# Softmax weights left unnormalised in the first attention steps, fewer TensorE array forms, and another order of the last matmuls

## The chip, the cores and the metric

One core of one Trainium2 chip runs the whole program. The metric is the device time of one execution in microseconds, shown as the median of several runs. A profiled execution has a time of its own, and a span from its first to its last instruction.

## The reference

Three blocks follow one another in float32: attention over 4 x 8 heads of 576 positions, with a causal window of 128 and a linear bias by distance; a feed-forward block with a softmax and a layer norm inside (SoLU); and a gated one.

```python
def _attn_ref(q, k, v):                       # (4, 8, 576, 64)
    scores = scale * np.matmul(q, k.transpose(0, 1, 3, 2))
    mask = (rel >= 0) & (rel < window)        # window = 128
    scores = np.where(mask, scores + bias[None], -1000000000.0)
    scores = scores - np.max(scores, axis=-1, keepdims=True)
    attn = np.exp(scores)
    attn = attn / (np.sum(attn, axis=-1, keepdims=True) + 1e-09)
    return np.matmul(attn, v)

def _moe_ref(x, w_in, w_out, g_ln):           # x (2304, 512), w_in (512, 1024)
    h = x @ w_in
    sm = softmax(h)
    solu = h * sm
    ln = (solu - mu) / np.sqrt(var + 1e-06) * g_ln
    return ln @ w_out

def _moe2_ref(x, w_gate, w_val, w_out):       # w_gate (512, 1536)
    g = x @ w_gate
    return g * sigmoid(g) * (x @ w_val) @ w_out
```

The weights of the two feed-forward blocks arrive as 64-bit words and are decoded to float32 on the chip.

## The kernel before

Every float32 product with a weight is made of three matmuls: both operands are split into a high and a low part (`high`, L267, and `low`, L271), and high x low, low x high and high x high are summed in PSUM (`HALVES`).

**Attention** runs in 20 steps (`steps`, 4 batches of 5 query tiles; the fifth has 64 rows). A step has four pairs of heads; a pair is one unit. For each pair of units `score` (L428) issues a block of small matmuls on 64 x 32 parts of the array. `attend` (L468) then takes a unit through the row maximum with the bias (VectorE, L488), two exponentials (ScalarE, L493) whose row sums are written beside them, their inverse (VectorE, L498 and L499), the scaling of the weights by it (`normalize`: ScalarE L504 or GpSimd L506), two transposes on TensorE (L524), a copy of these to SBUF (`pt`, L531 and L534) and, for two units at a time, the matmuls with the values (`values`, L566), on halves of 64 columns of the array. Keys reach over two tiles: one product is with the tile before (`vt`), one with the difference of the two (`vd`, made by `differ`, L410). In fifth tiles the transposes and the products with the difference use 64 rows of the array. The result (`px`, in a PSUM bank) is split into high and low, which are the feature tiles of the next block.

**The first feed-forward block** needs both weights decoded: `decode` (L319) takes a piece through ScalarE (L306, L310), VectorE (L311, L312), GpSimd (L314), and its split (L268, L272 or L274). `up` (L657) multiplies a feature tile by the first weight in two halves; `flip` (L719) turns the normalised tile, by TensorE or, for tiles 4 to 13, by a DMA for which `halves_of` first separates the 16-bit halves of the words; `down1` (L771) multiplies by the second weight. The matmuls of both have line L653.

**The second feed-forward block** uses seven products per block of weights (`products`, L992, matmuls at L1007). At its end `prepare` (L1095) makes operands out of stored results, `steps_of` (L1152) sums them over six chunks into PSUM (L1169), and `drain` (L1178) adds the finished sums to the output tiles (L1183) and stores them. There are six such passes; each goes chunk by chunk, and in a chunk product by product.

**The order** on every engine is fixed when the program is built. Each of these functions is a generator that hands operations to an `Emitter` (L105); it keeps a planned time for every engine and takes the operation that can start first, by rank among those that could start at once. An operation may name several engines; the one that would end first, with a bias (`B_DVE`, `B_ACT`), is taken. Offsets (`O_...`, `R_...`, `PW_...`) shift ranks. An engine name with a plus marks a port that VectorE and GpSimd share in the plan. From the planned time `TOGETHER` on, TensorE work that uses parts of the array (`form` 1 and 2) is held back in favour of plain matmuls while fewer than `LEAST` such operations are ready and none has waited `PATIENCE` ns. On the chip each engine takes its instructions in the written order and waits on semaphores.

Of the kernel before, what the change touches and what calls it, by code (L numbers as in the profile page):

```python
# [44 lines left out]
PLB = 2  # L45
PTB = 4
# [4 lines left out]
R_FLIP = 0.751  # L51
R_DOWN = 3.0
PW_IN = [-0.63, -0.23, -0.29, -0.28, 0.25, 0.17, 0.43, 0.28]
# [5 lines left out]
O_MAX = 0.0  # L59
O_EXP = -0.005  # L60
O_INV = 0.0
O_TURN = 0.136
O_PT = -1.188
O_VAL = 0.0
O_X = 0.316
# [4 lines left out]
O_LN = -0.416  # L70
# [4 lines left out]
TOGETHER = 96722.643  # L75
PATIENCE = 36.086
# [151 lines left out]
def attention_then_two_ffns(ctx: ExitStack, tc: tile.TileContext, qk, v, w_in, w_out, g_ln, w2, ident_d, base_d, tri_d, out):  # L228
# [145 lines left out]
    def load(c):  # L374
# [19 lines left out]
        loaded[c] = yield dma(vt[c][0:n], v[b, t * P:t * P + n, :], 262144)  # L394
# [15 lines left out]
    def differ(c):  # L410

        n = P if steps[c][1] < 4 else 64
        yield vd_s
        vd[c] = at.tile([P, DM], F32, tag="vd", bufs=VDB, name="vd")
        yield prepped[c][1]
        x = yield ([(POOL, t_pool(DM), lambda: nc.gpsimd.tensor_sub(vd[c][0:n], vt[c][0:n], vt[c - 1][0:n])),
                    (DVEP, t_dve(DM), lambda: nc.vector.tensor_sub(vd[c][0:n], vt[c][0:n], vt[c - 1][0:n]))],
                   [loaded[c], loaded[c - 1]])
# [4 lines left out]
    px_of, pts = {}, {}  # L423
# [43 lines left out]

    def attend(u):  # L468
# [23 lines left out]
        for j, d in enumerate(ds):  # L492
            ex.append((yield (ACT, 93 + t_act(P, True, True), lambda j=j: nc.scalar.activation(  # L493
                e[0:n, j], e[0:n, j], AF.Exp, bias=st[0:n, j:j + 1], scale=-1.0,
                accum_out=sc[0:n, j:j + 1]), [d, ds[0]], 0.0, O_EXP)))

# [4 lines left out]
        def normalize(eng):  # L501
# [6 lines left out]
        x = yield (DVE, 360, invert, ex, 0.0, O_INV)  # L508
        em.give(bank_s, x, k)
        x = yield ([(DVEP, t_dve(2 * P), lambda: normalize(nc.vector)),  # L510
                    (ACT, 2 * (93 + t_act(P)), lambda: normalize(nc.scalar)),
                    (POOL, t_pool(2 * P), lambda: normalize(nc.gpsimd))], [x], 0.0, O_INV)
# [14 lines left out]
        em.give(e_s, x)  # L527
        w = 2 * n
        ys = []
        if t:  # L530
            ys.append((yield (DVE, t_dve(w), lambda: nc.vector.tensor_tensor(  # L531
                pt[0:n, 1, :, 0:n], tp[0:n, :, 0:n], tri[0:n, 1, 0:n].unsqueeze(1).to_broadcast([n, 2, n]), ALU.mult),
# [21 lines left out]
        if t:  # L554
            yield differed[c]

        def values():
            todo = [(r, late) for r in units for late in ((1, 0) if t else (0,))]
            if t == 4:
                todo.sort(key=lambda x: -x[1])  # L560
            for r, late in todo:
                kp = n if late else P
                for j in range(2):
                    h = 2 * r + j
                    src = vd[c] if late else vt[c - 1] if t else vt[c]
                    nc.tensor.matmul(px[j * 64:(j + 1) * 64, r, 0:n], src[0:kp, h * 64:(h + 1) * 64],  # L566
                                     pts[c * NPAIR + r][0:kp, late, j, 0:n], start=r == 0 and (late == 1 or t == 0), stop=(late == 0),
                                     skip_group_check=True)

        values.form = 2  # L570
        x = yield (PE, 100 + 450 * len(units), values, [loaded[c]], 0.0, O_VAL)
# [9 lines left out]
        if t:  # L581
            em.give(v_s, x)
            em.give(vd_s, x)
        t0 = b * S + t * P
        done = 0
        last = []
        while done < n:
# [6 lines left out]
            src = px[:, :, done:done + w]  # L594
            y = yield (high(hi, src, 4 * w, False), [x], 0.0, O_X)
            y = yield (low(lo, src, hi, 4 * w, False), [y], 0.0, O_X)
# [7 lines left out]
        em.give(bank_s, y, px_of[c])  # L604
# [345 lines left out]
    def part_y(p, kk):  # L950
        yield opened2[p]
        if p == 1:
# [4 lines left out]
        x = yield (DMA, 2600.0, lambda: nc.sync.dma_start_transpose(  # L957
            r.rearrange("p (a h) t -> p a (h t)", a=2).bitcast(U16), src), (), 2000.0)
# [97 lines left out]
    ob, ob_ok = {}, [[Done() for _ in range(HB)] for _ in range(2 * NPR)]  # L1056
    t4_done = [[Done() for _ in range(HB)] for _ in range(NPR)]
# [37 lines left out]
    def prepare(k, i):  # L1095
# [45 lines left out]
        else:  # L1141
            x1 = yield add(r[:, 1], r[:, 1], r[:, 0], ALU.subtract, [x])
            x4 = yield add(r[:, 2], r[:, 2], t2, ALU.subtract, [x])
            sa = yield from split(0, 3, r[:, 1:4], [x1, x4])
            ends = [sa]
# [6 lines left out]
    def steps_of(k):  # L1152
# [3 lines left out]
        for i in range(HB):  # L1156
            yield ob_ok[k][i]
            yield wo_ok[i]
            for j, name in enumerate(PASS[half]):
                for q in range(2):  # L1160
                    if i == 0:
                        bk[name, q] = yield bank_s
                    o = banks[bk[name, q]][:, 0:NH]
                    c = PROD[name][0] * 256 + q * P
                    w = wo[i][:, :, c:c + P]

                    def f(o=o, w=w, j=j, i=i):
                        for m, (b, a) in enumerate(HALVES):
                            nc.tensor.matmul(o, w[:, b], ob[k, i][a][:, j], start=i == 0 and m == 0, stop=i == HB - 1 and m == 2)  # L1169

                    x = yield (PE, 3 * 0.455 * NH, f)
                    last[name, q] = x
            em.give(w2_s, x)
# [108 lines left out]
```

## Time and profile before

| | |
|---|---|
| median of 3 runs | 747.87 us (747.63 to 748.11) |
| the profiled execution | 744.56 us |
| its span, first to last instruction | 742.8 us |
| TensorE busy | 708.3 us (95%), 5084 matmuls |
| VectorE, ScalarE, GpSimd busy | 544.5 (73%), 469.9 (63%), 257.0 us (35%) |
| chain that ended last | TensorE 34% of the span |

PE is TensorE, PEld its weight load, DVE VectorE, ACT ScalarE, POOL GpSimd, SP the engine that issues the transfers. Busy shares are means over stages; a stage is read from its own window. A matmul in float32 of an attention product stands in the trace as two records.

### The profile page before, as it was taken

How to read it: one execution, taken by the hardware profiler on the slowest of the kernel's cores; microseconds unless marked ns; L12 is line 12 of the kernel's file. 1: busy time of each engine (PE TensorE's matmuls, PEld its weight loads, DVE VectorE, ACT ScalarE, POOL GpSimd, SP SyncE). 2: the span in 40 equal slices, each digit the busy share in tenths (PEclk: the TensorE clock that was granted, in tenths of full speed). 3: DMA queues.
4: the chain of work that ended last, by engine and by line, in shares of the span. 5: the costliest groups of instructions: out<-in, count | busy, mean ns of one | idle time of the engine just before them, and what ended most of it. 6: DMA issues, size and time to landing. Idle time of an engine off the chain costs nothing. (4 is left out here: it accounts for less than half of the span.)

```text
span 742.8 us, 14409 instructions
## 1 busy us (share of the span) xinstructions
PE 708.3 (95%) x5084; PEld 627.8 (85%) x5084; DVE 544.5 (73%) x1499; ACT 469.9 (63%) x1146; POOL 257.0 (35%) x268
## 2 busy tenths in 40 slices
PE   3879979999999999998999999999999999999997
PEld 1547757767787888888999999999999999999997
DVE  4778985667566654989978776876763699887975
ACT  7899996777777675786657555555553564442531
POOL 3686674454565554550034231221310000110200
PEclk9999999999999999999999999999999999999999
DMA  8763216354454327255564445643431788786851
GB/s 269 219 194 112 86 52 171 107 143 108 115 150 115 93 72 171 72 141 122 162 206 163 163 135 181 188 165 145 151 108 64 273 344 295 253 288 203 288 181 64
DMA packets 92329, 121.34 MB, mean 163 GB/s; under 512 B 46432, under 2 KB 59104, under 8 KB 92256
## 3 DMA queue, kind: packets, MB, share of 16 engines
q1 hardware_dynamic: 92256, 120.42, 51.6%
q8 instruction: 40, 0.66, 0.4%
q14 instruction: 33, 0.27, 0.1%
HBM read 76.09 MB, written 34.34 MB: 149 GB/s over the span
## 5 line engine op out<-in xcount | busy, mean ns | idle before, releaser
L1007 PE MATMUL bank<-yt,w 128*128 128x384 f32 x1008 | 183.5, 337 | 3.2 <-ACT t L1028 2.2
L1007 PEld LDWEIGHTS bank<-yt,w 128*128 128x128 f32 x1008 | 175.4, 188 | 6.4 <-ACT set L1028 2.8
L314 POOL TENSOR_TENSOR db<-db,dw 128x512 int32<-128x512 int32 x52 | 71.1, 1369 | 187.4 <-DVE db L312 144.4
L1169 PE MATMUL bank<-w,wo 128*128 128x384 f32 x756 | 132.9, 336 | 0.0
L1169 PEld LDWEIGHTS bank<-w,wo 128*128 128x128 f32 x756 | 132.3, 188 | 0.2 <-DVE w L272 0.2
L653 PE MATMUL bank<-wout,lnT 128*128 128x512 f32 x432 | 102.3, 392 | 0.0
L1007 PE MATMUL bank<-shared,w 128*128 128x384 f32 x504 | 96.0, 340 | 1.5 <-ACT set L1028 0.8
L653 PEld LDWEIGHTS bank<-wout,lnT 128*128 128x128 f32 x432 | 80.4, 188 | 17.2 <-issue 0.5
L1007 PEld LDWEIGHTS bank<-shared,w 128*128 128x128 f32 x504 | 87.2, 188 | 5.8 <-ACT set L1028 2.5
L653 PE MATMUL bank<-shared,shared 128*128 128x512 f32 x288 | 82.9, 418 | 1.6 <-ACT shared L268 1.6
L493 ACT ACTIVATE e<-e,st 128x128 f32<-128x128 f32 (+1 forms) x160 | 62.6, 401 | 14.7 <-DVE st L488 12.5
L653 PEld LDWEIGHTS bank<-shared,shared 128*128 128x128 f32 x288 | 51.9, 195 | 13.6 <-ACT shared L268 2.4
L506 POOL TENSOR_TENSOR e<-e,st 128x256 f32<-128x256 f32 (+1 forms) x66 | 40.8, 622 | 42.4 <-DVE st L499 31.1
L268 ACT CAST w<-t 128x768 fp32r<-128x768 f32 (+2 forms) x33 | 26.4, 806 | 42.3 <-DVE t L1123 26.7
L306 ACT ACTIVATE dw<-dw 128x512 int32<-128x512 uint32 x52 | 35.1, 675 | 14.5 <-DMA dw<-w 11.5
L488 DVE CUSTOM_DVE_ANT_0 e<-bank,bias 128x128 f32<-128x128 f32 (+1 forms) x160 | 38.5, 282 | 4.9 <-PE bank L454 2.7
L454 PE MATMUL bank<-keys,raw 64*32 64x160 f32 (+1 forms) x1152 | 32.5, 322 | 9.2 <-DMA keys<-qk 9.1
L1033 DVE TENSOR_TENSOR set<-set,bank 128x384 f32<-128x384 f32 x34 | 18.8, 552 | 30.3 <-PE bank L1007 23.3
L268 ACT CAST w<-db 128x512 fp32r<-128x512 f32 (+1 forms) x48 | 27.0, 565 | 20.7 <-POOL db L314 16.1
L524 PE MATMUL bank<-ident,e 128*128 128x128 f32 (+1 forms) x160 | 28.8, 291 | 11.3 <-POOL e L506 4.8
L653 PE MATMUL bank<-shared 128*128 128x512 f32 x144 | 38.9, 392 | 0.0
L524 PEld LDWEIGHTS bank<-ident,e 128*128 128x128 f32 (+1 forms) x160 | 18.3, 146 | 24.2 <-POOL e L506 8.7
(109 smaller groups left out, 1237.9 us busy)
## 6 DMA issues: line engine op xcount, KB each, us to landing
dw<-w SPq DMA_DIRECT2D x36, 512.0 KB, 3.9
t<-ascr SPq DMA_DIRECT2D x21, 768.0 KB, 5.5
ascr<-set SPq DMA_DIRECT2D x34, 384.0 KB, 2.6
later<-ascr SPq DMA_DIRECT2D x15, 768.0 KB, 5.4
wo<-wscr SPq DMA_DIRECT2D x6, 896.0 KB, 6.8
lscr<-pl SPq DMA_DIRECT2D x20, 256.0 KB, 2.3
raw<-qk SPq DMA_DIRECT2D x19, 256.0 KB, 3.4
yscr<-ys SPq DMA_DIRECT2D x18, 256.0 KB, 2.2
```

The costliest lines, as they stand in the source:

```text
L268: return [(ACT, t_act(n, sbuf), lambda: nc.scalar.copy(hi, src)), (DVEP if sbuf else DVE, t_dve(n, sbuf), lambda: nc.vector.tensor_copy(hi ...
L306: r = yield (ACT, t_act(512), lambda: nc.scalar.activation(a, lw, AF.Copy, scale=2.0 ** -29), (), 0.0, O_DEC)
L314: x = yield (POOL, t_pool(512), lambda: nc.gpsimd.tensor_tensor(b.bitcast(I32), b.bitcast(I32), a, ALU.add), [x, r], 0.0, O_DEC)
L454: nc.tensor.matmul(banks[ks[r]][i:i + Q, o:o + w], raw[c][rows, 2 * qd + j, i:i + Q], kt[rows, 2 * qd + j, k0:k0 + w], start=True, stop=True)
L488: d = yield (DVE, t_dve(P), lambda j=j: nc.vector.tensor_tensor_reduce(e[0:n, j], sc[0:n, j * 256:j * 256 + P], bias[0:n, 2 * pr + j, bs], ...
L493: ex.append((yield (ACT, 93 + t_act(P, True, True), lambda j=j: nc.scalar.activation(e[0:n, j], e[0:n, j], AF.Exp, bias=st[0:n, j:j + 1], ...
L506: eng.tensor_tensor(e[0:n], e[0:n], st[0:n, 6:8].unsqueeze(2).to_broadcast([n, 2, P]), ALU.mult)
L524: nc.tensor.transpose(tp[:, j, 0:n], e[0:n, j], ident[0:n, 0:n])
L653: nc.tensor.matmul(o, terms[m][0], terms[m][1], start=(m == 0), stop=(m == len(terms) - 1))
L1007: nc.tensor.matmul(o, l, r, start=first and m == 0, stop=m == 5, skip_group_check=True)
L1033: g2 = yield (DVE, t_dve(NH), lambda: nc.vector.tensor_add(t[:, 1], t[:, 1], sb), [x3, u2], 0.0, O_FREE)
L1169: nc.tensor.matmul(o, w[:, b], ob[k, i][a][:, j], start=i == 0 and m == 0, stop=i == HB - 1 and m == 2)
```

## The change

Four parts, all in one program.

In the first four steps (`SUMS = 4`) the exponentials are transposed and multiplied with the values as they are. The row sums of a step are collected in one SBUF tile (`rs`); after the last unit, two small VectorE operations invert all eight. TensorE multiplies each column of inverses, repeated over 64 columns, with the identity: that spreads them over the layout of `px` in a second bank. The bank is copied to SBUF (`rec`), multiplied by `px`, and the split into high and low reads `rec`. The bank of the scores is given back after the maximum instead of after the inverse.

Fifth tiles use full 128 x 128 transposes and value matmuls over 128 rows; the host pads `v` with zeros to 640 rows per batch, and whole tiles are loaded.

In the last pass, the last two chunks go product by product instead of chunk by chunk, and their operands are split part by part.

The planner's constants change: grouping on TensorE starts at 76.1 instead of 96.7 us and holds back for 517 instead of 36 ns; ranks of seven of the eight pieces of the first weight move by -0.08; copies of halves on GpSimd and transposing DMAs get other planned costs; and some offsets.

```diff
+SUMS = 4
-R_FLIP = 0.751
+R_FLIP = 0.741
-PW_IN = [-0.63, -0.23, -0.29, -0.28, 0.25, 0.17, 0.43, 0.28]
+PW_IN = [-0.63, -0.31, -0.37, -0.36, 0.17, 0.09, 0.35, 0.2]
-O_MAX = 0.0
+O_MAX = 0.338
-O_INV = 0.0
-O_TURN = 0.136
+O_INV = 0.814
+O_TURN = -0.064
-O_X = 0.316
+O_X = 0.674
-O_LN = -0.416
+O_LN = -0.345
-TOGETHER = 96722.643
-PATIENCE = 36.086
+TOGETHER = 76077.562
+PATIENCE = 517.289
...
     def turn_by_dma(dst, src, nbytes, deps=()):
-        return (DMA, max(445.0, nbytes / 250.0), lambda: nc.sync.dma_start_transpose(dst, src), deps, 2200.0)
+        return (DMA, 1000.0 + 1.56 * src.shape[0], lambda: nc.sync.dma_start_transpose(dst, src), deps,
+                1300.0 + min(900.0, nbytes / 290.0))
...
-                (POOL, t_pool(2 * n), lambda: nc.gpsimd.tensor_copy(dst, words))]
+                (POOL, 450.0 + 0.3 * 2 * n, lambda: nc.gpsimd.tensor_copy(dst, words))]
...
-        loaded[c] = yield dma(vt[c][0:n], v[b, t * P:t * P + n, :], 262144)
+        loaded[c] = yield dma(vt[c], v[b, t * P:(t + 1) * P, :], 262144)
...
+        if c < SUMS:
+            em.give(bank_s, ds[1], k)
...
+            for j, d in enumerate(ds):
+                ex.append((yield (ACT, 93 + t_act(P, True, True), lambda j=j: nc.scalar.activation(
+                    e[0:n, j], e[0:n, j], AF.Exp, bias=st[0:n, j:j + 1], scale=-1.0,
+                    accum_out=rs[c][0:n, 0, 2 * pr + j:2 * pr + j + 1]), [d, ds[0]], 0.0, O_EXP)))
...
-                nc.tensor.transpose(tp[:, j, 0:n], e[0:n, j], ident[0:n, 0:n])
+                nc.tensor.transpose(tp[:, j], e[:, j], ident)
...
+            y = yield (DVE, 160, lambda: nc.vector.tensor_scalar_add(rs[c][0:n, 1], rs[c][0:n, 0], 1e-9), (), 0.0, O_INV)
+            inv.append((yield (DVE, 190, lambda: nc.vector.reciprocal(rs[c][0:n, 2], rs[c][0:n, 1]), [y], 0.0, O_INV)))
+            sum_of[c] = yield bank_s
...
-            if t == 4:
-                todo.sort(key=lambda x: -x[1])
...
-                    nc.tensor.matmul(px[j * 64:(j + 1) * 64, r, 0:n], src[0:kp, h * 64:(h + 1) * 64],
-                                     pts[c * NPAIR + r][0:kp, late, j, 0:n], start=r == 0 and (late == 1 or t == 0), stop=(late == 0),
+                    nc.tensor.matmul(px[j * 64:(j + 1) * 64, r, 0:n], src[:, h * 64:(h + 1) * 64],
+                                     pts[c * NPAIR + r][:, late, j, 0:n], start=r == 0 and (late == 1 or t == 0), stop=(late == 0),
...
+                        nc.tensor.matmul(sums[j * 64:(j + 1) * 64, r, 0:n], rs[c][0:n, 2, 2 * r + j:2 * r + j + 1].to_broadcast([n, 64]),
+                                         ident[0:n, 0:n], start=True, stop=True, skip_group_check=True)
...
+        if c < SUMS:
+            yield rec_s
+            rec = at.tile([P, NPAIR, P], F32, tag="rec", bufs=1, name="rec")
+            sums = banks[sum_of[c]].rearrange("p (r q) -> p r q", r=NPAIR)
+            em.give(rs_s, x)
+            y = yield ([(ACT, t_act(4 * n, False), lambda: nc.scalar.copy(rec[:, :, 0:n], sums[:, :, 0:n])),
+                        (DVE, t_dve(4 * n), lambda: nc.vector.tensor_copy(rec[:, :, 0:n], sums[:, :, 0:n]))], [x], 0.0, O_X)
+            em.give(bank_s, y, sum_of[c])
+            x = yield (DVE, t_dve(4 * n), lambda: nc.vector.tensor_mul(rec[:, :, 0:n], rec[:, :, 0:n], px[:, :, 0:n]), [x, y], 0.0, O_X)
+            em.give(bank_s, x, px_of[c])
+        src_x, in_sbuf = (rec, True) if c < SUMS else (px, False)
...
+            if k == 2 * NPR - 1 and i >= HB - 2:
+                ends = []
+                for j, d in enumerate((x1, x4, x)):
+                    ends.append((yield from split(j, 1, r[:, 1 + j], [d])))
+                    chain(ends[j], ob_part[i][j])
...
+        todo = [(i, j, q) for i in range(HB) for j in range(len(names)) for q in range(2)]
+        if k == 2 * NPR - 1:
+            todo.sort(key=lambda x: x if x[0] < HB - 2 else (HB - 2, x[1], x[2], x[0]))
```

## Rows read from the trace of the kernel before

**Rows 1.** Windows: stage, length, busy us (count) of PE PEld DVE ACT POOL, clock, DMA
```profile
18.00:34.00 16.00, 13.62 (x167) 8.23 (x168) 12.15 (x58) 14.33 (x52) 10.77 (x11) 1.00 0.81 243
34.00:52.00 18.00, 12.95 (x184) 7.95 (x184) 14.65 (x73) 15.23 (x51) 12.88 (x12) 0.98 0.51 154
52.00:112.00 60.00, 55.63 (x574) 40.61 (x573) 50.61 (x209) 55.13 (x173) 42.89 (x49) 0.98 0.32 99
112.00:300.00 188.00, 186.81 (x1666) 147.47 (x1664) 115.94 (x518) 135.09 (x408) 99.35 (x120) 1.00 0.46 122
```

**Rows 2.** Groups of lines, 18 to 52 us: busy us, mean ns | idle before, releasers
```profile
L524 PE MATMUL bank<-ident,e 128*128 128x128 f32 x26 | 7.8, 379 | 5.6 <-ACT e L504 4.0 <-POOL e L506 1.6
...
L504 ACT ACTIVATE e<-e,st 128x128 f32<-128x128 f32 x14 | 4.8, 397 | 0.0
...
L506 POOL TENSOR_TENSOR e<-e,st 128x256 f32<-128x256 f32 x6 | 3.9, 659 | 1.2 <-ACT bias L405 0.8 <-DVE st L499 0.4
...
L272 DVE TENSOR_TENSOR shared<-bank,shared 128x512 fp32r<-128x512 f32 x3 | 2.1, 684 | 0.9 <-ACT shared L268 0.9
L499 DVE RECIPROCAL st<-st 128x2 f32<-128x2 f32 x12 | 2.0, 166 | 0.4
...
L498 DVE TENSOR_SCALAR st<-bank 128x2 f32<-128x2 f32 x12 | 1.8, 152 | 0.1
...
L268 ACT CAST shared<-bank 128x512 fp32r<-128x512 f32 x3 | 1.7, 582 | 0.0
```

**Rows 3.** Timeline of TensorE, 0 to 60 us: start, length, what [idle before]
```profile
17.93 1.32 PE L454 MATMUL bank<-keys,raw 64*32 64x160 f32 x32 [1.84 <-DMA keys<-qk]
...
37.43 0.77 PE L454 MATMUL bank<-keys,raw 64*32 64x160 f32 x32
...
52.08 2.79 PE L653 MATMUL bank<-shared,shared 128*128 128x512 f32 x6
...
57.93 1.64 PE L653 MATMUL bank<-shared,shared 128*128 128x512 f32 x6
```

**Rows 4.** Timeline of GpSimd, end of the first weight
```profile
49.67 2.50 POOL L274 TENSOR_TENSOR shared<-db,shared 128x512 fp32r<-128x512 f32 x2
```

**Rows 5.** Windows of one microsecond: the clock behind 52 us
```profile
52.00:53.00 1.00, 1.00 (x4) 0.89 (x4) 0.64 (x5) 0.67 (x5) 1.00 (x2) 0.50 0.79 295
```

**Rows 6.** Timeline of TensorE: value matmuls among plain ones, 75 to 285 us
```profile
75.17 0.66 PE L566 MATMUL bank<-pt,v 128*64 128x128 f32 x8
...
79.55 0.66 PE L566 MATMUL bank<-pt,v 128*64 128x128 f32 x8
...
281.22 0.45 PE L566 MATMUL bank<-pt,vd 64*64 64x64 f32 x8
```

**Rows 7.** Timeline of TensorE: transposes of a fifth tile and a full one
```profile
137.97 0.71 PE L524 MATMUL bank<-ident,e 64*128 64x64 f32 x8
138.61 0.73 PE L653 MATMUL bank<-shared,shared 128*128 128x512 f32 x2
...
215.34 1.04 PE L524 MATMUL bank<-ident,e 128*128 128x128 f32 x8
216.13 1.62 PE L653 MATMUL bank<-shared,shared 128*128 128x512 f32 x6
```

**Rows 8.** Timeline of TensorE: four matmuls before an attention block, and before plain ones
```profile
161.09 1.08 PE L653 MATMUL bank<-shared 128*128 128x512 f32 x4
162.10 0.44 PE L566 MATMUL bank<-pt,vd 128*64 128x128 f32 x4
...
179.03 1.09 PE L653 MATMUL bank<-shared 128*128 128x512 f32 x4
179.96 5.61 PE L653 MATMUL bank<-wout,lnT 128*128 128x512 f32 x24
```

**Rows 9.** Timeline of the end, TensorE and VectorE
```profile
727.75 10.57 PE L1169 MATMUL bank<-w,wo 128*128 128x384 f32 x59
...
735.71 3.80 DVE L1183 TENSOR_TENSOR later<-later,bank 128x384 f32<-128x384 f32 x8 [1.19 <-PE bank L1169]
```

More of the change, by code (lines that the diff above doesn't have):

```diff
@@ L410, in differ @@
     def differ(c):
-        n = P if steps[c][1] < 4 else 64
         yield vd_s
@@ L422, in attention_then_two_ffns @@
     e_s, pt_s, st_s, px_s = Slots(EB), Slots(PTB), Slots(EB), Slots(PXB)
-    px_of, pts = {}, {}
+    px_of, pts, sum_of = {}, {}, {}
+    rec_s = Slots(1)
+    rs, rs_s, summed = {}, Slots(3), [Done() for _ in range(NU)]
     halved = [Done() for _ in range(NU)]
@@ L466, in score, with give_e @@
                 em.give(keys_s, x)
+    rs_there = [Done() for _ in range(NS)]
+    def give_e(x, y):
+        yield x
+        yield y
+        em.give(e_s, x if x.time > y.time else y)
     def attend(u):
@@ L491, in attend @@
             ds.append(d)
[L492 to L495, printed above, removed]
         def invert():
@@ L523, in flip_p @@
             for j in range(2):
-                nc.tensor.transpose(tp[:, j, 0:n], e[0:n, j], ident[0:n, 0:n])
+                nc.tensor.transpose(tp[:, j], e[:, j], ident)
         x = yield (PE, 218, flip_p, ident_ok, 0.0, O_TURN)
-        em.give(e_s, x)
+        if c < SUMS and got is not None:
+            em.start(give_e(x, got), 0.0)
+        else:
+            em.give(e_s, x)
         w = 2 * n
@@ L555, in attend @@
             yield differed[c]
+        inv = []
+        if c < SUMS and pr == NPAIR - 1:
+            for r in range(NPAIR):
+                yield summed[c * NPAIR + r]
+            y = yield (DVE, 160, lambda: nc.vector.tensor_scalar_add(rs[c][0:n, 1], rs[c][0:n, 0], 1e-9), (), 0.0, O_INV)
+            inv.append((yield (DVE, 190, lambda: nc.vector.reciprocal(rs[c][0:n, 2], rs[c][0:n, 1]), [y], 0.0, O_INV)))
+            sum_of[c] = yield bank_s
         def values():
             todo = [(r, late) for r in units for late in ((1, 0) if t else (0,))]
-            if t == 4:
-                todo.sort(key=lambda x: -x[1])
             for r, late in todo:
-                kp = n if late else P
                 for j in range(2):
@@ L1056, in attention_then_two_ffns @@
     ob, ob_ok = {}, [[Done() for _ in range(HB)] for _ in range(2 * NPR)]
+    ob_part = {i: [Done() for _ in range(3)] for i in (HB - 2, HB - 1)}
     t4_done = [[Done() for _ in range(HB)] for _ in range(NPR)]
@@ L1155, in steps_of, with f @@
         bk, last = {}, {}
-        for i in range(HB):
-            yield ob_ok[k][i]
-            yield wo_ok[i]
[L1159 to L1173, printed above, removed]
+        names = PASS[half]
+        todo = [(i, j, q) for i in range(HB) for j in range(len(names)) for q in range(2)]
+        if k == 2 * NPR - 1:
+            todo.sort(key=lambda x: x if x[0] < HB - 2 else (HB - 2, x[1], x[2], x[0]))
+        last_of = {x[0]: n for n, x in enumerate(todo)}
+        for z, (i, j, q) in enumerate(todo):
+            name = names[j]
+            yield ob_part[i][j] if k == 2 * NPR - 1 and i >= HB - 2 else ob_ok[k][i]
+            yield wo_ok[i]
+            if i == 0:
+                bk[name, q] = yield bank_s
+            o = banks[bk[name, q]][:, 0:NH]
+            c = PROD[name][0] * 256 + q * P
+            w = wo[i][:, :, c:c + P]
+            def f(o=o, w=w, j=j, i=i):
+                for m, (b, a) in enumerate(HALVES):
+                    nc.tensor.matmul(o, w[:, b], ob[k, i][a][:, j], start=i == 0 and m == 0, stop=i == HB - 1 and m == 2)
+            x = yield (PE, 3 * 0.455 * NH, f)
+            last[name, q] = x
+            if last_of[i] == z:
+                em.give(w2_s, x)
         gone[k].settle(0.0)
```

56 lines of the change are left out of this document (38 added, 18 removed).

## Prediction

> **What bounds the kernel now.** I read the busy times by stage first [rows 1]. From 112 to 300 us TensorE works 186.81 of 188.00 us and the others at most 135.09: there only its own instructions count. From 18 to 52 us it is different: TensorE works 13.62 of 16 and 12.95 of 18 us, so 7.4 us are lost, while ScalarE is busy 29.6 of 34, VectorE 26.8 and GpSimd 23.7. From 52 to 112 us ScalarE (55.13 of 60) and TensorE (55.63) are both nearly full. This is the ramp: attention of the first steps and the decoding of two weights share three engines, and TensorE waits.
>
> The groups of lines between 18 and 52 us say for what [rows 2]: 5.6 us of idle stand in front of the transposes of the softmax weights (L524), 4.0 ended by the normalising on ScalarE (L504), 1.6 by that on GpSimd (L506). Before 18 us the scores of the second step waited for their keys' transfer, 1.84 us [rows 3]: what the first step wins before that is not passed on.
>
> Next, what ends the ramp. The second half of the first up-projection starts at 52.08 [rows 3], when the last low halves of its weight leave GpSimd (49.67 + 2.50 = 52.17 [rows 4]). Until then nearly all of TensorE's work is attention.
>
> Two rates show in the TensorE timeline. A score block of 32 records took 1.32 us at 17.93 and 0.77 at 37.43; six matmuls of the up-projection took 2.79 us at 52.08 and 1.64 at 57.93 [rows 3]. For the last pair the granted clock is beside it: 0.50 in 52 to 53 us [rows 5], the lower of the two levels, after a stretch in which TensorE mostly waited. For the first 32 us the column says 1.00, yet the rows have the long durations; I go by the durations.
>
> **The change, part by part.**
>
> *Normalising, steps 0 to 3.* Sixteen pairs of heads lose two small VectorE operations and one scaling. In steps 1 to 3 (the 12 of L498 and L499) that is 14 ScalarE instructions (7 pairs), 4.8 us, and 5 pairs on GpSimd at 0.659 us, 3.3 us; the group's sixth instruction belongs to step 0. VectorE loses 12 x (0.152 + 0.166) = 3.8 us [rows 2]. The transposes then follow the exponentials directly. The gain is at most the 5.6 us of idle that normalising ended, and at least nothing, if each transpose then waits as long for the exponential. I take 4.0: ScalarE, 87% busy in the stretch, loses 4.8 and gets about 2.4 back (below), so the decoding behind it ends some 2.4 us sooner, and about as much again of the idle is latency (inverse, scaling and two hops between engines). If ScalarE were not the cover, that 4.0 would be the latency part alone, 1.6.
>
> *The clock.* If TensorE no longer idles before 51 us, the half-rate stretch behind it goes. The six matmuls at 52.08 would win 2.79 - 1.64 = 1.15 us, the value matmuls behind them a little: between 0 and -1.3. I take -1.0.
>
> *What is added per step.* Eight matmuls that spread the reciprocals over 64 rows each, in the shape of the value matmuls. A first attention tile shows its eight value matmuls as two rows of eight records; such a row is busy for 0.66 us [rows 6], so eight matmuls cost at most 1.3 us at full rate and about twice that before 32 us. For four steps the upper bound is 5.3 us, the lower nothing if they fall into the 7.4 us of idle. Then a copy from PSUM (ScalarE, 0.582) and a product (VectorE, 0.684), both 128 x 512 [rows 2]: ScalarE +2.4 us, VectorE +2.8, and 0.3 per step for two small operations. The low halves of these four tiles now read SBUF and may go to GpSimd at 1.25 us [rows 4]: +5.0 there against 5.9 taken off (9 pairs at 0.659). Most of this lies before 52 us beside idle; the fourth step's values lie behind, where ScalarE and TensorE are full. I take +1.0, one such block.
>
> The feature tiles come about 1.3 us later by copy and product. I cost this at nothing: the second up-projection starts at 57.93 [rows 3], behind the weight, not behind tiles 0 to 2; without that cover it would be 1.3 us for a tile. The spreading matmuls are a new wait: for the inverse on VectorE, after the fourth unit's exponentials. Behind them in TensorE's queue stand the next step's transposes and scores. But the value matmuls ahead of them wait for that same unit's transposes and copies, which end later than its exponentials by two engines' work, so the inverse should be there: 0.
>
> *Fewer array forms, fifth tiles.* Transposes of 64 x 128 become 128 x 128: eight took 137.97 to 138.61 = 0.64 us, the large ones 215.34 to 216.13 = 0.79 [rows 7]: 4 x 0.15 = +0.6. The value matmuls keep 64 columns. What a change of form costs: four matmuls of the same form are followed after 179.96 - 179.03 = 0.93 us, four before an attention block after 162.10 - 161.09 = 1.01 [rows 8], so 0.08 for going in. I take four changes saved per batch at 0.08 in part, -0.4: net +0.2 (between -0.7 and +0.6).
>
> *Grouping on TensorE.* The emitter begins to group from 76 us and holds an attention block back up to 517 instead of 36 planned ns. Between the block at 79.55 and that at 281.22 [rows 6] I count 25 runs of attention blocks among plain matmuls; 15 steps lie there. Going in, a first matmul that is slower and coming out together are about 0.25 us (three times 0.08). At most 10 runs can go, -2.5; none, 0. I take four: -1.0, all on the bound engine.
>
> *Copies planned on GpSimd, transposes by DMA planned longer, other offsets.* These move work among engines that wait for TensorE after 112 us [rows 1]: GpSimd 99.35 of 188 us busy, ScalarE 135.09. I take 0; if the cover is gone it costs one copy's delay here and there: -0.5 to +1.
>
> *The end.* VectorE does eight additions from 735.71 for 3.80 us and ends at 739.5, while TensorE's last row ends 727.75 + 10.57 = 738.3 [rows 9]. That row has 59 matmuls, 0.179 us each; a chunk is six products of three, 3.2 us. By product, the last two chunks spread the finished sums over 6.4 instead of 3.2 us, so VectorE keeps up and only one addition (3.80 / 8 = 0.48) is left: 738.3 + 0.5 = 738.8, -0.7. The last chunk's first part is then needed 3.2 - 0.5 = 2.7 us earlier, and its halves are cut in three so that it can be. Between -1.2 and, if the parts come late, +0.5.
>
> **Sum.** 744.56 (the profiled execution; its span is 742.8, 1.76 lie around it) - 4.0 - 1.0 + 1.0 + 0.2 - 1.0 - 0.7 = 739.1. The median of the runs is 747.87, 3.31 above the profiled execution: 742.4. All of it must pass through 112 to 735 us, where TensorE's order is full; I see nothing there that waits for a fixed time.
>
> **Rivals.** *The first rate ends sooner* (17 in 100). In 18 to 34 us TensorE is busy 13.62 of 16 us at the lower rate, so it is near its own bound there. Without the waits, and with the added matmuls, it may reach the full rate some 8 us earlier; half of its work in them, 8 x 0.85 / 2 = 3.4 us, is saved on top: 739.0. Against it: nothing in the trace tells when the rate rises but that it came with dense work at 32 us.
>
> *The ramp gives nothing* (16 in 100). GpSimd sees 5.9 us go and up to 5.0 come, and ends the weight as before at about 52 us: terms one and two are gone, 742.4 + 5.0 = 747.4, no measurable change. For it: GpSimd's low halves are the last thing before 52.08. Against it: before them it sat idle, and VectorE and ScalarE fed it late. The Trainium skill ("SBUF — State Buffer", section "Who interferes with whom") speaks for this rival: it has a VectorE instruction with two SBUF inputs and a GpSimd instruction that reads SBUF shut each other out, and the four subtractions change from a PSUM source to two SBUF ones. By that rule even those left on VectorE would stop GpSimd, 0.68 us each and 2.7 in all; the sum would be 745.1.
>
> *Holding back makes attention late* (12 in 100; the slower side). Of the 25 runs, each may be held 517 - 36 = 0.48 us longer in the written order; TensorE takes its queue in order, so whatever follows in it waits when the plan was wrong. If half of that becomes idle time, 25 x 0.24 = 6.0 us and the grouping's 1.0 is lost too: 749.4. It decides from 5.5 / 25 = 0.22 us of new idle per run. For it: in 76 to 112 us the other engines are full and results come late. Against: after 112 us TensorE has spare matmuls ready.
>
> **Chances.** The forecast has 55 in 100, its own range 740 to 744.7 (half of the first term either way, and one of the small ones). 0.2% (1.5 us) is about what a measurement of this kernel can tell from no change. Faster: forecast, first rival and half of the second's neighbourhood, 0.78; within: the rest of the second and a part of the third, 0.13; slower: 0.09. The range from 737 to 748 leaves out the third rival and a little of the first.
>
> **What would show it.** No normalising (L504, L506) for the first 16 pairs, and less than 2 us of idle before L524 in 18 to 52 us; the last low half of the first weight at about 48; no granted 0.5 after 50 us; four longer value blocks; fewer than 25 runs of attention blocks; after TensorE's end one addition. Wrong it would be if the weight still ends at 52, or if TensorE's idle time in 76 to 300 us grows by more than 3 us.

## The result, and the profile after

The changed kernel took 738.02 us (median of 4 runs, 737.61 to 739.38); the kernel before took 747.75 us on the same chip (4 runs, 747.60 to 748.11). The ratio is 0.9872, with a 95% interval from 0.9848 to 0.9896: 9.7 us faster. The profiled execution took 738.17 us, its span is 736.4. It lies at the changed kernel's median, while that of the kernel before lay 3.2 us below its own: between the two profiles the difference is 6.4 us, and only these can be explained from the traces. One execution of the kernel before (1386 us) and one of the kernel without the first part (1396 us) took nearly twice as long as the others; the medians and ranges here leave them out.

Line numbers move: the transposes are now L552, the scores L457, the values L601, the spreading matmuls L609, the first block's matmuls L706, the last pass L1232 and its additions L1247.

First the page's row of TensorE and then the windows, of after, with columns as in [rows 1]; the windows of 2 us below them are for the clock, the last column but two.

```profile
PE 707.0 (96%) x5148; PEld 632.9 (86%) x5148; DVE 545.3 (74%) x1489; ACT 459.2 (62%) x1127; POOL 261.4 (36%) x268
```

```profile
18.00:34.00 16.00, 12.95 (x182) 8.74 (x182) 10.11 (x48) 12.12 (x36) 12.86 (x10) 0.79 0.80 248
34.00:52.00 18.00, 16.92 (x253) 12.88 (x253) 15.03 (x63) 16.35 (x60) 12.90 (x10) 1.00 0.73 229
52.00:112.00 60.00, 55.06 (x567) 41.80 (x567) 53.62 (x221) 54.69 (x173) 46.23 (x51) 1.00 0.29 92
112.00:300.00 188.00, 186.59 (x1678) 150.10 (x1677) 118.08 (x521) 131.65 (x409) 106.80 (x126) 1.00 0.46 123
...
24.00:26.00 2.00, 0.24 (x2) 0.05 (x2) 2.00 (x9) 1.13 (x4) 1.28 (x1) 0.83 1.09 359
26.00:28.00 2.00, 2.00 (x35) 1.12 (x35) 1.55 (x9) 1.48 (x6) 2.00 (x3) 0.50 1.13 316
...
32.00:34.00 2.00, 1.88 (x16) 1.24 (x8) 1.64 (x9) 1.53 (x7) 1.93 (x2) 0.97 0.17 49
52.00:54.00 2.00, 2.00 (x10) 1.43 (x9) 1.52 (x9) 1.97 (x10) 1.21 (x2) 1.00 0.37 131
```

Against [rows 1], one stage stands out: from 34 to 52 us TensorE works 16.92 instead of 12.95 of 18 us. The other stages move by less than 1 us. Over the whole span TensorE is idle 736.4 - 707.0 = 29.4 us, before 742.8 - 708.3 = 34.5; so 5.1 of the 6.4 us are idle time that went (4.0 of them between 34 and 52), and 1.3 are busy time that went, although 64 records were added.

The clock shows what the table of stages hides. It stands at the lower level, 0.50, after 26 us and is back near 1.00 at 32 to 34; the later stretch [rows 5] is gone. The groups of lines from 18 to 52 us, of after, as in [rows 2]:

```profile
L552 PE MATMUL bank<-ident,e 128*128 128x128 f32 x25 | 7.0, 344 | 4.0 <-ACT e L524 3.7
L609 PE MATMUL bank<-ident,rs 128*64 128x128 f32 x64 | 5.1, 311 | 0.9 <-DVE rs L592 0.9
...
L634 DVE TENSOR_TENSOR rec<-rec,bank 128x512 f32<-128x512 f32 x3 | 2.1, 684 | 4.6 <-ACT rec L631 4.6
L631 ACT COPY rec<-bank 128x512 f32<-128x512 f32 x3 | 1.7, 562 | 0.0
L591 DVE TENSOR_SCALAR rs<-rs 128x8 f32<-128x8 f32 x3 | 1.6, 546 | 0.0
```

The idle time in front of the transposes went from 5.6 to 4.0 us only, and it now ends on the exponentials (L524) instead of the normalising. A new wait stands behind it: 0.9 us for the inverse (L592). The timelines of TensorE, GpSimd and VectorE, of after:

```profile
20.93 1.80 PE L457 MATMUL bank<-keys,raw 64*32 64x160 f32 x64
23.90 0.33 PE L552 MATMUL bank<-ident,e 128*128 128x128 f32 x1 [1.17 <-ACT e L524]
25.98 0.48 PE L552 MATMUL bank<-ident,e 128*128 128x128 f32 x1 [1.76 <-ACT e L524]
26.39 1.32 PE L457 MATMUL bank<-keys,raw 64*32 64x160 f32 x32
...
32.80 1.64 PE L706 MATMUL bank<-shared,shared 128*128 128x512 f32 x6
...
35.30 1.04 PE L609 MATMUL bank<-ident,rs 128*64 128x128 f32 x16
...
44.17 1.04 PE L609 MATMUL bank<-ident,rs 128*64 128x128 f32 x16
...
49.78 1.09 PE L609 MATMUL bank<-ident,rs 128*64 128x128 f32 x16 [0.85 <-DVE rs L592]
50.80 2.11 PE L706 MATMUL bank<-shared,shared 128*128 128x512 f32 x8
```

```profile
48.11 1.27 POOL L276 TENSOR_TENSOR shared<-db,shared 128x512 fp32r<-128x512 f32 x1 [1.24 <-ACT shared L270]
```

```profile
48.14 1.27 DVE L591 TENSOR_SCALAR rs<-rs 128x8 f32<-128x8 f32 x1
...
49.53 0.19 DVE L592 RECIPROCAL rs<-rs 128x8 f32<-128x8 f32 x1
```

The weight's last low half ends at 48.11 + 1.27 = 49.38 (before 52.17, [rows 4]). Eight matmuls take 2.11 us, at the full rate; six took 2.79 before [rows 3]. But they start at 50.80, not at 49.4, because the spreading matmuls stand ahead of them and wait for the inverse. Its first half, a 128 x 8 addition, began 0.03 us after the GpSimd instruction and ended with it.

Busy time between 34 and 52 us is not yet time won: three blocks of spreading, 1.04, 1.04 and 1.09 us, lie in that window, 3.2 of the 4.0 us. What the ramp won is read better at a point that has the same work behind it: the end of the first up-projection, after its 24 matmuls. Windows up to this point, of before, of after and of the kernel with the old grouping (below), whose first 560 TensorE records come in the same order as those of after:

```profile
0.00:57.41 57.41, 37.61 (x456) 22.90 (x456) 37.98 (x186) 47.16 (x159) 34.09 (x37) 0.97 0.71 222
0.00:53.67 53.67, 38.16 (x520) 26.25 (x521) 37.03 (x165) 42.17 (x137) 31.20 (x29) 0.94 0.74 238
0.00:51.10 51.10, 37.42 (x520) 26.05 (x521) 37.19 (x165) 42.09 (x137) 31.19 (x29) 0.97 0.80 250
```

The 456 records are the same in all three; the 64 further ones are the spreading. The change passes the point 3.7 us sooner: TensorE's idle time went down by 4.3 us (19.80 to 15.51), the spreading added 5.1 us, and everything else took about 4.5 us less (rows overlap a little, so this split is rough). The same order in another execution passes it 2.6 us sooner still, so one profile gives the ramp's gain only to within that.

The end, of after: TensorE's last row ends at 602.42 + 130.40 = 732.82, and one addition follows it, where eight stood in [rows 9]. The span ends 3.58 us after TensorE, before 742.8 - 738.33 = 4.47.

```profile
731.80 0.56 DVE L1247 TENSOR_TENSOR later<-later,bank 128x384 f32<-128x384 f32 x1 [0.51 <-PE bank L1232]
732.86 0.56 DVE L1247 TENSOR_TENSOR later<-later,bank 128x384 f32<-128x384 f32 x1 [0.51 <-PE bank L1232]
```

### The profile page after: what moved, and what is told of

Same layout as the page of the kernel before. It is cut to its first block, busy times and chain, and to the rows that moved or that the text cites. A ratio compares the mean times of both kernels' runs of the same rounds, so it can differ in the third digit from the quotient of the medians.

```text
span 736.4 us, 14536 instructions
## 1 busy us (share of the span) xinstructions
PE 707.0 (96%) x5148; PEld 632.9 (86%) x5148; DVE 545.3 (74%) x1489; ACT 459.2 (62%) x1127; POOL 261.4 (36%) x268
## 5 line engine op out<-in xcount | busy, mean ns | idle before, releaser
L1232 PE MATMUL bank<-w,wo 128*128 128x384 f32 x756 | 132.8, 336 | 0.0
L1232 PEld LDWEIGHTS bank<-w,wo 128*128 128x128 f32 x756 | 132.4, 188 | 0.0
L706 PE MATMUL bank<-wout,lnT 128*128 128x512 f32 x432 | 102.5, 392 | 0.0
L706 PEld LDWEIGHTS bank<-wout,lnT 128*128 128x128 f32 x432 | 80.4, 188 | 16.7 <-issue 0.2
L706 PE MATMUL bank<-shared,shared 128*128 128x512 f32 x288 | 78.4, 404 | 0.8 <-ACT shared L270 0.8
L533 ACT ACTIVATE e<-e,st 128x128 f32<-128x128 f32 (+1 forms) x128 | 49.6, 401 | 21.5 <-DVE st L498 18.5
L706 PEld LDWEIGHTS bank<-shared,shared 128*128 128x128 f32 x288 | 51.4, 189 | 12.7 <-issue 1.9
L270 ACT CAST w<-t 128x384 fp32r<-128x384 f32 (+2 forms) x35 | 26.7, 772 | 40.0 <-DVE t L1176 28.0
L511 POOL TENSOR_TENSOR e<-e,st 128x256 f32<-128x256 f32 (+1 forms) x55 | 33.4, 621 | 21.1 <-ACT e L533 9.6
L706 PE MATMUL bank<-shared 128*128 128x512 f32 x144 | 38.8, 391 | 0.0
L314 DVE SCALAR_TENSOR_TENSOR db<-dw,db 128x512 uint32<-128x512 uint32 x52 | 38.2, 740 | 0.6
L457 PE MATMUL bank<-keys,raw 64*32 64x160 f32 (+1 forms) x1152 | 30.3, 316 | 8.6 <-DMA keys<-qk 6.7
L552 PE MATMUL bank<-ident,e 128*128 128x128 f32 x160 | 30.1, 296 | 8.7 <-ACT e L524 5.6
```

The lines of the kernel that those rows point to most:

```text
L270: return [(ACT, t_act(n, sbuf), lambda: nc.scalar.copy(hi, src)), (DVEP if sbuf else DVE, t_dve(n, sbuf), lambda: nc.vector.tensor_copy(hi ...
L314: x = yield (DVEP, t_dve(512), lambda: nc.vector.scalar_tensor_tensor(b, hw, 0x80000000, b, ALU.bitwise_and, ALU.bitwise_or), [x], 0.0, O_DEC)
L457: nc.tensor.matmul(banks[ks[r]][i:i + Q, o:o + w], raw[c][rows, 2 * qd + j, i:i + Q], kt[rows, 2 * qd + j, k0:k0 + w], start=True, stop=True)
L552: nc.tensor.transpose(tp[:, j], e[:, j], ident)
L706: nc.tensor.matmul(o, terms[m][0], terms[m][1], start=(m == 0), stop=(m == len(terms) - 1))
```

## The experiments

Medians are compared with the kernel before on the same chip; parts of the change with the changed kernel through these ratios. In profile times: before 744.56, after 738.17.

**The kernel before, again** (no edit), for the 3 us between its profile and its median.

> The kernel before, unchanged, profiled anew. The changed kernel's profiled execution lay at its median (738.17 against 738.02), that of the kernel before 3.2 us under its own (744.56 against 747.75). Theory: the kernel before has executions that differ in the first 60 us, where TensorE's rate changes, and the profiled one was a short one; a new profile then shows a time between 744 and 748, and where it is above 746 the half-rate stretches or the idle of TensorE before 60 us are longer by about as much. Rival: a profile of this kernel always comes out 3 us short; then the new profile shows 744.5 +- 0.5 again beside timed runs of 747.7.

It took 747.59 us (745.02 to 749.09, 12 runs), ratio 0.9997 (0.9978 to 1.0015). Its profiled execution, 745.02, was again the shortest of its runs. With the first, two profiles of two lie about 3 us short, so the rival is not refuted: 745.02 is at the edge of its 744.5 +- 0.5. The runs of the kernel before lie between 744.56 and 752.98, the four of the changed kernel within 1.8 us. Whether the 3.31 us that I added to the sum are chance within a wide spread or belong to profiles of this kernel is open; they are no constant that a changed kernel keeps. Why the spread is wide was not settled. The mean granted clock of an execution does not sort it: 744.95 us came at 0.990, 752.98 at 0.988.

**The change without its first part.**

```diff
-SUMS = 4
+SUMS = 0
```

> Only the first part undone: all steps normalise as before, the rest of the change stays. Theory (the ramp was relieved by taking normalising out): most of the gain goes, 744 us (747.75 less about 1.75 for 7 fewer runs of attention blocks, 1.0 for the fifth tiles and 0.9 at the end), with 4 us or more of TensorE idle back before 60 us. Rival (the new order and constants did it, not the normalising): 740 us or less.

752.51 us (749.97 to 755.91, 10 runs), ratio 1.0068 (1.0045 to 1.0092): slower than before, beyond any theory. Windows and GpSimd timeline of this kernel:

```profile
34.00:52.00 18.00, 11.60 (x175) 7.45 (x175) 13.15 (x57) 13.60 (x48) 11.94 (x13) 0.81 0.41 129
```

```profile
54.42 1.27 POOL L276 TENSOR_TENSOR shared<-db,shared 128x512 fp32r<-128x512 f32 x1
```

With normalising in the ramp, the weight ends at 55.69 and TensorE works 1.35 us less than in [rows 1] in the same stage. The other parts do not stand by themselves: in a kernel whose first steps still normalise, they lose about 5 us together (747.60 before on this chip).

**The first part alone**, in the kernel before with its constants, fifth tiles and end.

```diff
+SUMS = 4
...
+        if c < SUMS:
+            em.give(bank_s, ds[1], k)
...
```

> Only the first part of the change: unnormalised weights in four steps (and whole padded tiles of v loaded); constants, grouping, fifth tiles and end as in the kernel before. Theory (parts add up): 741.5 as with the old constants, +0.9 for the end, +1.0 for the fifth tiles: 743.4, with executions that lie within 2 us of each other. Rival (the part needs the new order to pay): 746 or more.

741.31 us (741.15 to 741.54), ratio 0.9922 (0.9891 to 0.9952): 5.3 us less than before on its chip. Its profile, 741.15, is 3.4 under that of before. Windows of this kernel:

```profile
34.00:52.00 18.00, 16.93 (x238) 12.76 (x234) 14.74 (x64) 16.32 (x58) 13.53 (x11) 1.00 0.66 204
52.00:112.00 60.00, 54.34 (x569) 39.48 (x568) 53.58 (x223) 57.15 (x173) 45.27 (x49) 1.00 0.28 92
```

TensorE's whole rise between 34 and 52 us is there, and the four runs lie within 0.4 us. What is left for the other three parts is 741.15 - 738.17 = 3.0 us of profile. None of it is won in the ramp. This kernel passes the end of the first up-projection sooner than after does, with as many records:

```profile
0.00:51.63 51.63, 37.08 (x520) 25.62 (x520) 37.38 (x165) 42.26 (x136) 30.60 (x28) 0.97 0.78 248
```

That is 5.8 us sooner than before, where the profile as a whole gains 3.4. From this point to the end of the span it needs 739.4 - 51.63 = 687.8 us, before 742.8 - 57.41 = 685.4, after 736.4 - 53.67 = 682.7.

**All constants as before**, the other parts kept.

```diff
-O_MAX = 0.338
+O_MAX = 0.0
-O_INV = 0.814
+O_INV = 0.0
...
-PATIENCE = 517.289
+PATIENCE = 36.086
...
```

> The changed kernel with all constants of the order as before: ranks of the weight's pieces, offsets, planned costs of copies and transposing transfers, and the grouping (from 96.7 us, 36 ns). Theory: only the grouping is lost, 738.0 + 1.8 = 740 us, and the ramp is as in the changed kernel. Rival (the constants carry the ramp's gain): 743 us or more.

741.46 us (741.16 to 742.41), ratio 0.9919 (0.9893 to 0.9945), profile 741.32: as the first part alone. So nearly all of the 3 us comes with the constants, and they act behind the ramp: this kernel passes the end of the first up-projection at 52.08 and needs 739.5 - 52.08 = 687.4 us from there. Three runs each put one group of the constants back.

**Grouping as before.**

```diff
-TOGETHER = 76077.562
-PATIENCE = 517.289
+TOGETHER = 96722.643
+PATIENCE = 36.086
```

> The changed kernel with the grouping of TensorE's attention blocks as before (from 96.7 us, held back 36 ns). Theory: 18 runs of attention blocks become about 25 again, at 0.25 us each, 739.8 us, and the ramp before 76 us is the same. Rival (holding back is not what counts): 738.0.

738.35 us (737.77 to 739.01), ratio 0.9881 (0.9855 to 0.9908): nothing that can be measured.

**Planned costs of copies and transposing DMAs as before.**

```diff
...
-                (POOL, 450.0 + 0.3 * 2 * n, lambda: nc.gpsimd.tensor_copy(dst, words))]
+                (POOL, t_pool(2 * n), lambda: nc.gpsimd.tensor_copy(dst, words))]
...
```

> The changed kernel with the planned costs of the copies on GpSimd and of the transposing transfers as before. With all constants as before 741.5 was measured, with the grouping alone as before 738.4. Theory (the ranks and offsets carry these 3 us): 738.0 to 738.8. Rival (the planned costs do): 740.5 or more.

736.51 us (735.28 to 737.67), ratio 0.9846 (0.9813 to 0.9880): the lowest time of all. Its interval overlaps that of the change; the planned costs give nothing that can be measured, and may cost some 1.5 us.

**The ranks of the weight's pieces as before.**

```diff
-PW_IN = [-0.63, -0.31, -0.37, -0.36, 0.17, 0.09, 0.35, 0.2]
+PW_IN = [-0.63, -0.23, -0.29, -0.28, 0.25, 0.17, 0.43, 0.28]
```

> The changed kernel with the ranks of the first weight's eight pieces as before. Theory (the earlier pieces bring the up-projection forward, and that is the larger part of the 3 us that the constants gave): 739.5 or more. Rival (the offsets within attention do it, or it is spread): 738.0 to 738.8.

738.02 us (736.36 to 739.25), ratio 0.9868 (0.9838 to 0.9897): nothing. What remains of the constants are the offsets (`O_MAX`, `O_INV`, `O_TURN`, `O_X`, `O_LN`, `R_FLIP`). A sign of them stands in the groups of 112 to 300 us. Scores of full tiles, 480 records each, of before, of after and of the kernel with the old grouping, in this order:

```profile
L454 PE MATMUL bank<-keys,raw 64*32 64x160 f32 x480 | 13.5, 301 | 0.1
```

```profile
L457 PE MATMUL bank<-keys,raw 64*32 64x160 f32 x480 | 12.0, 300 | 0.0
```

```profile
L457 PE MATMUL bank<-keys,raw 64*32 64x160 f32 x480 | 12.0, 300 | 0.0
```

The same records take 1.5 us less. With the offsets of after, the scores of a step mostly go in one row of 64 records; I count 8 such rows and 8 of 32 after 75 us (one of these broken by a wait), where before has 5 and 13, and three of 16. Runs of attention blocks (scores and values between other matmuls, transposes left out), counted in one way for every kernel from 75 us on: before 24, the first part alone 22, all constants old 22, after 17, grouping old 16, ranks old 17, costs old 18. So `TOGETHER` and `PATIENCE` do not join the blocks, and neither do ranks or planned costs alone; by elimination it is the offsets. From the end of the first up-projection, after and the four kernels that keep its offsets and its end (grouping, costs, ranks or fifth tiles old) need 682.6 to 684.9 us, the one with all constants old 687.4. No run put the offsets back by themselves, and that groups carry the gain only together is not excluded.

**Fifth tiles as before.**

```diff
-                nc.tensor.transpose(tp[:, j], e[:, j], ident)
+                nc.tensor.transpose(tp[:, j, 0:n], e[0:n, j], ident[0:n, 0:n])
...
```

> The changed kernel with fifth tiles as before: transposes of 64 x 128, value matmuls with the difference over 64 rows, differences last. Theory from the two traces: a whole fifth-tile cycle lost 0.25 us, so four of them cost 1.0 us and the time is 739.0. Rival (the prediction's sizing, 0.2 us in the other direction): 737.8.

738.06 us (737.36 to 738.20), ratio 0.9875 (0.9849 to 0.9901). The larger forms and the saved changes of form are worth nothing that can be measured.

**The end as before.**

```diff
...
-        if k == 2 * NPR - 1:
-            todo.sort(key=lambda x: x if x[0] < HB - 2 else (HB - 2, x[1], x[2], x[0]))
...
```

> The changed kernel with the last pass chunk by chunk as before. Theory: 738.0 + 0.9 = 738.9 us, and the time from TensorE's last matmul to the end of the span is 4.5 us again, as before, against 3.6 in the changed kernel. Rival (the end is set by the last store whatever the order): the same 738.0 and no difference in that time.

739.31 us (737.79 to 740.88), ratio 0.9890 (0.9862 to 0.9918). Its span ends 4.45 us after TensorE, as before; so 0.9 us of the profile is the end's, though the medians differ by less than their intervals.

**Eight steps instead of four.**

```diff
-SUMS = 4
+SUMS = 8
```

> The changed kernel with eight instead of four steps unnormalised. Steps 4 to 7 lie from 52 to 112 us, where TensorE is 92% busy. Theory (each further step costs TensorE about 1 us for the spreading matmuls there, while only about half of its 4.9 us of idle can come back): between 738 and 741 us, not below 737. Rival (normalising is what every attention step waits for): 736 or less.

745.45 us (742.68 to 748.19), ratio 0.9968 (0.9942 to 0.9993): four more steps cost about 7 us (0.9872 with four). The window from 52 to 112 us of this kernel, and the waits of TensorE there: us in total, times, longest:

```profile
52.00:112.00 60.00, 55.15 (x611) 42.16 (x610) 49.71 (x189) 55.03 (x166) 43.12 (x44) 0.97 0.30 87
```

```profile
PE bank L811 <- ACT rec L631: 1.7, 1, 1.7
PE bank L811 <- DVE st L498: 0.8, 1, 0.8
...
PE bank L706 <- ACT rec L631: 0.6, 1, 0.6
```

Where ScalarE is 92% busy, the copy from PSUM (L631) becomes a wait of its own, 2.3 us in all. It does not explain the loss: TensorE is idle there no longer than after the change (60 - 55.15 = 4.85, 60 - 55.06 = 4.94). Over the whole profile (746.87 us) TensorE is busy 712.9 us, 5.9 more than after; the 64 further spreading records take 3.9 of them, as the theory had it. From 300 to 600 us its idle time is 7.6 us, after 3.9; what causes that is open. The spread is wide again, 5.5 us.

**The normalising's load kept, nobody waiting for it.** The changed kernel, with an inverse and a scaling for each of the first 16 pairs on spare tiles whose contents nothing uses.

```diff
...
+            y = yield (DVE, 360, old_invert, ex, 0.0, O_INV)
+            yield ([(DVEP, t_dve(2 * P), lambda: old_scale(nc.vector, 0)),
+                    (ACT, 2 * (93 + t_act(P)), lambda: old_scale(nc.scalar, 1)),
+                    (POOL, t_pool(2 * P), lambda: old_scale(nc.gpsimd, 2))], [y], 0.0, O_INV)
...
```

> The changed kernel with the load of the normalising put back but not its place in the chain: for the first 16 units the two small VectorE operations and one scaling (VectorE, ScalarE or GpSimd, by the same planned costs) run on spare tiles that nobody waits for. Theory 'load' (the three engines were too full in the ramp): the time goes most of the way back, 743 us or more, and TensorE's busy time in 34 to 52 us falls from 16.9 towards 13. Theory 'chain' (each unit's latency from exponential to transposes was too long): 740 or less, and TensorE's busy time in 34 to 52 us stays above 16.

756.52 us (755.62 to 757.39), ratio 1.0116 (1.0089 to 1.0144). A window, a row of the groups from 18 to 64 us, and the waits of TensorE in the same stretch, of this kernel:

```profile
34.00:52.00 18.00, 15.43 (x235) 11.61 (x234) 17.66 (x66) 15.71 (x52) 12.80 (x13) 1.00 0.52 162
```

```profile
L481 DVE TENSOR_SCALAR tiny<-tiny 128x2 f32<-128x2 f32 x12 | 7.8, 646 | 0.2
```

```profile
PE bank L631 <- DVE rs L614: 6.9, 2, 5.1
PE bank L574 <- ACT e L542: 3.4, 4, 1.2
```

The time is that of the load: with no one waiting for the scaled weights, the gain is gone and more. TensorE's busy time from 34 to 52 us, 15.43, lies between the two theories. The size is overstated. The added addition reads SBUF and took 646 ns, where the one that was removed reads PSUM and took 152 [rows 2]: VectorE got 12 x 0.494 = 5.9 us more than had been taken off. TensorE waited 6.9 us for the inverse of the row sums, which stands in VectorE's order among these; that is a wait that neither theory had, so the run does not separate load from chain.

**The kernel before, with TensorE kept busy.** Small matmuls of the identity, whose result nothing uses, in the planned gaps from 9 to 56 us; one PSUM bank is set aside for them.

```diff
...
+                if 9000.0 < t < FILL_TO and self.fill:
+                    self.fill(int((t - self.free("PE")) / 160.0))
...
```

> The kernel before with extra matmuls of the identity, whose result is not used, put into TensorE's queue wherever the plan has it idle between 9 and 56 us (one PSUM bank is set aside for them until the fourth step's values are done). Theory (its median lies 3 us above its best executions because TensorE falls to the lower rate in some of them): fewer half-rate stretches before 60 us, a median of 745 or less, executions within 2.5 us where those of the kernel before spread over 6. Rival (the rate is a symptom, the waits set the time): the median stays at 747 to 749 or rises by what the extra matmuls cost.

759.31 us (757.61 to 767.94), ratio 1.0176 (1.0136 to 1.0217): a miss. A window, and the timeline of TensorE, of this kernel:

```profile
18.00:34.00 16.00, 16.00 (x173) 13.36 (x172) 5.77 (x26) 8.43 (x30) 6.97 (x6) 1.00 0.48 143
```

```profile
19.58 6.08 PE L357 MATMUL bank<-ident 128*128 128x64 f32 x28
25.58 1.32 PE L469 MATMUL bank<-keys,raw 64*32 64x160 f32 x32
...
33.38 0.77 PE L469 MATMUL bank<-keys,raw 64*32 64x160 f32 x32
```

TensorE is never idle from 18 to 34 us, yet a block at 25.58 still has the slow duration, after 6 us of filling. The filling stands in TensorE's written order ahead of the scores, so it holds them back. What a higher rate alone would give in the ramp was not measured.

## Why the prediction was right, and where its sum was off

It said 742.4 us, from 737 to 748, and faster; 738.02 was measured. On the profiles the sum was 739.1 and 738.17 was found. The missing 4.4 us are thus 0.9 of the sum and 3.5 of the offset, the "3.31 above the profiled execution", which is about -0.15 after. The measured time lies outside the forecast's own range, 740 to 744.7, and inside the wide one. That the sum came within 0.9 us is in part luck: the added work cost TensorE 5.1 us where 1.0 was forecast, its other work in the ramp took about 4.5 us less where the clock's term had 1.0, and these two misses nearly cancel.

*Normalising (-4.0 forecast).* The place was right: 16.92 - 12.95 = 4.0 us of idle went between 34 and 52 us, and the first part alone brings all of it. To the end of the first up-projection 4.3 us of idle went, and the ramp is 3.7 us shorter; normalising, clock and added work had -4.0 in sum. The step "less than 2 us of idle before the transposes" was wrong (4.0): the idle time between 18 and 34 us stayed and grew (16 - 12.95 = 3.05, before 2.38). There the transposes now wait for the exponentials. The weight ended 2.8 us sooner in this execution, at 49.38, where 48 was forecast; in the seven other kernels with four unnormalised steps it ended between 46.81 and 48.54. Whether the other engines' load or the latency was relieved is not shown, and so neither is the split into 2.4 and 1.6: without the first part both come back (weight at 55.69), and the load kept put a new wait before TensorE.

*The clock (-1.0).* The stretch at 52 us went, as said. The term was too small: up to the end of the first up-projection, all but the spreading took about 4.5 us less. Of that, 1.15 is the term's own price, 1.04 are six matmuls of the first half (1.64 us at 32.80, before 2.68 at 31.83), and 0.84 the scores at 20.93; the rest was not traced. The first half of the up-projection, of before:

```profile
31.83 2.68 PE L653 MATMUL bank<-shared,shared 128*128 128x512 f32 x6
```

A part of the rival "first rate ends sooner" came true too: the 64 records at 20.93 took 1.80 us, where twice 1.32 would be 2.64. It was lost again after 1.17 and 1.76 us of idle time, and the block at 26.39 took 1.32. From 18 to 34 us TensorE got through 182 records, 16 of them the new ones at 19 us, and through 167 before [rows 1]: nothing was won in that stage.

*Added work (+1.0).* Sixteen records of spreading take 1.04 us at the full rate, under the 1.3 of the bound. But all 64 take 5.1 us, near the upper bound of 5.3, and TensorE has to do them before the first up-projection ends; +1.0 was too small. The low halves of the four tiles all went to GpSimd, 1.26 to 1.87 us each. The step that failed is "the inverse should be there: 0". In the fourth step TensorE waited 0.85 us for it, and the first up-projection with it; in the seven other kernels with four unnormalised steps it was 0.83 to 0.85. I had priced the two small operations by rows that read PSUM; on SBUF the addition took 1.27 us beside GpSimd. The Trainium skill ("SBUF — State Buffer", section "Who interferes with whom") says that a `tensor_scalar` can take the port pair that VectorE and GpSimd share, and that whoever comes second is blocked for the whole instruction of the other. The trace agrees: the addition starts at 48.14, the GpSimd instruction at 48.11, and they end within 0.03 us of each other.

*Fifth tiles (+0.2).* Nothing measurable either way; right.

*Grouping (-1.0), other offsets (0).* Fewer runs came, 17 after 24, and 1.5 us of score time went with them. But the old grouping constants give 16 runs and the same time; the offsets brought it. So the two terms were put on the wrong constants, and together they were too small: -1.0 forecast, 2 to 3 us found (3.0 of profile against the first part alone with the end's 0.9 in it, 3.15 against all constants old), all of it behind the ramp. That it is the offsets is by elimination: no run changed them alone.

*The end (-0.7).* 4.47 to 3.58, -0.9; one addition behind TensorE, as said.

*The rivals.* "The ramp gives nothing" fell: the weight ends 2.8 us sooner, although the four low halves did come to GpSimd. None of them stayed on VectorE, so its price of 2.7 us was not put to the test. "Holding back makes attention late" fell: with the old holding the time is the same, and TensorE's idle time from 112 to 300 us is 1.41 us, before 1.19 (from 76 to 300 us 5.58, before 5.28). "The first rate ends sooner" came in part and did not last (above): 738.02 lies near its 739.0 by other ways.

## What to carry to other kernels

Work taken out of a stage where several engines feed the bound one is worth the idle time there, and the same edit in a full stage costs time: four steps gave 5.3 us alone, four more cost about 7. The constants of an order belong to the operations that they were found with: without the first part, the rest of this change lost about 5 us. To see what a ramp won, compare the times at a point with the same work behind it, in more than one execution: 4.0 us more of busy time in a window held 3.2 us of added work. Before a median is forecast from a profile, look how far the executions spread; an offset between the two need not carry over.

## What the runs showed of the hardware

A VectorE addition on a 128 x 8 tile in SBUF took from 158 to 1268 ns, of after; the 128 x 2 one that reads PSUM took 141 to 159, of before, both up to 60 us:

```profile
L591 DVE TENSOR_SCALAR rs<-rs x4: 158/186/1268, 17.7 to 48.1; 128x8 f32<-128x8 f32 x4
```

```profile
L498 DVE TENSOR_SCALAR st<-bank x20: 141/152/159, 9.9 to 55.3; 128x2 f32<-128x2 f32 x16, 64x2 f32<-64x2 f32 x4
```

In the eight other kernels with these additions, the one with the load kept left out, the longest took 1253 to 1269 ns: about the length of a GpSimd instruction on 128 x 512, 1.27 us. What decides for them is whether GpSimd is in the middle of an instruction. Over these nine traces and that of the load kept, all 47 additions on SBUF that began while a GpSimd instruction ran ended 0.02 to 0.05 us after that instruction; the 11 with GpSimd idle throughout took 155 to 169 ns. Of the 80 in the kernel before that read PSUM, 60 began beside a GpSimd instruction and took 141 to 161 ns all the same. The reciprocal behind the addition, also on SBUF, kept to 194 ns on average, of after. A tiny operation in front of TensorE can so cost as much as a large one of another engine.

And TensorE's higher rate was lost soon after it came, of after: 64 score records at 20.93 took 1.80 us, faster than the lower rate; idle stretches of 1.17 and 1.76 us between 22 and 26 us, with one transpose between them, were followed by a granted clock of 0.50 until near 32 us.
